# Loading a gated linear attention with MLP in single units, its weights through five shared staging tiles and in the order of use

## The chip, the cores and the metric

The kernel runs on one NeuronCore of a Trainium2 chip. The metric is the time of the device for one execution, in microseconds (us); before the change its median of three runs is 189.53 us (189.49 to 190.04).

The engines are called PE (TensorE, matrix products), PEld (its weight loads), ACT (ScalarE, exp, ln, silu), DVE (VectorE), POOL (GpSimd) and SP (SyncE, which here only issues transfers). A name with a q, such as SPq, is the engine's own queue of instructions.

## The reference

Two steps follow each other. The first is an attention with a decaying state, for 4 batches, 8 heads, 768 positions and 48 channels; the second is an MLP without biases on the 3072 rows of 384 numbers that the first one gives.

```python
f = 1.0 / (1.0 + np.exp(-f_logit))
for t in range(S):
    state = f[:, :, t, :, None] * state + np.einsum('bhd,bhe->bhde', k[:, :, t], v[:, :, t])
    y[:, :, t] = np.einsum('bhd,bhde->bhe', q[:, :, t], state)
x = y.transpose(0, 2, 1, 3).reshape(B * S, H * D)     # 3072 x 384
h = x @ w_in                                          # w_in 384 x 2048
out = (h / (1.0 + np.exp(-h))) @ w_out                # w_out 2048 x 384
```

All inputs and the output are float32 in memory; the matrix products run in bf16.

## The kernel before

**Units.** The sequence is cut into 6 chunks of 128 positions. A unit is one chunk of one batch with all 8 heads; there are 24, numbered chunk by chunk, so units 0 to 3 are the first chunk of the four batches. Two neighbouring units make a pair. A unit needs the state of unit u - 4 and nothing else of other units.

**A unit's way.** Its four inputs f, k, q, v are loaded (L485), 192 KB each, in pieces of 48 float32, which is 192 bytes. ACT makes the log of the gate (L492 exp, L494 ln). PE sums it along the chunk with a triangular matrix (`cs`, L565, and a small sum for the state, L569). ACT makes three exponentials of it (L572, L574, L576). POOL scales k (`ki`, L578) and casts v (`vb`, L580), DVE scales q (`qg`, L582). q and k are then transposed, on PE (`tq`, L588) with a copy by DVE (`qkc`, L590), or by a transposing DMA (`qkD`, L592); units from `turned` on take the DMA. PE multiplies k by q (`sc`, L599), DVE masks (`at`, L603), PE gives y from the state (L608) and the chunk (L612), DVE casts it (`yc`, L616). y is transposed on PE (`yT`, L620) and copied by DVE (`xc`, L622), or by a DMA (`xD`, L625); units from `y_turned` on take the DMA. The state is updated by PE (`d`, L630), DVE (`sd`, L635, L637) and POOL (`su`, L641), except in the last chunk.

**The MLP.** For units below `single` (6) the first product runs unit by unit (`m1`, L529, four groups j of 512 columns of w_in, 12 matmuls each, silu on L526); from there on in pairs (`mi`, L540, eight groups of 256 columns, silu on L536). The second product (`mo`, L551) is 16 matmuls a unit in four groups m, one for each quarter of w_out. For the first `halves` units it is cut in two sums, of which DVE adds the second to the first (L554, L557); the others are copied by L559. Rows are stored by a DMA (`so`, L562), issued from POOL for units below `store_sp` and from SP for the others. The results of both products take three banks of PSUM, the class `mlp`.

**The weights.** w_in comes in four pieces (`wi`, L505) by 512 columns, w_out in four pieces (`wo`, L510), each of 768 KB in float32. A piece is loaded into a staging tile and cast to bf16 by one engine (`ci`, `co`, L519 on ACT, L520 on DVE or POOL). Before, w_in has four staging tiles `ws` and w_out two of its own, `wt`.

**The order.** It is made when the program is built. `make_tasks` lists each step with its engine, an estimated duration and a priority: `base(u)` (unit number times `pace`) plus a rank of its kind from `CFG`; loads of the first units and of the weights have `... - 1000.0`, so that they come first, in the order of these numbers (`w_at` for the eight weight pieces). `schedule` simulates the five engines and the transfers, and on each free engine starts the ready step of the least priority whose buffers (`SLOTS`) are free. Its SP holds back while more than `DEPTH` of transfers is queued. ACT changes between the table of exp and ln and that of silu by the rules of `hold_` and `keep_` (L294); each change is a table load (L677). `planned` runs this twice and returns one list, which `emit` writes down; on the chip each engine runs its part of it in that order, and waits by semaphores. Where the plan leaves PE idle in the first 60 us, `idle` puts matmuls of a blank tile (L652), which keep its clock up.

The loads of units 0 to 3 are single before, those of later pairs are one transfer of 384 KB for both units:

```python
groups = [(u0,), (u0 + 1,)] if P < 2 else [(u0, u0 + 1)]
```

With `w_at` from 2.93 to 4.0 and loads at `us[0] + 0.25 * len(us) * n - 1000.0`, the weights of before start among the loads of unit 2's end and unit 3.

Of the kernel before, what the change touches and what calls it, by code (L numbers as in the profile page):

```python
# [24 lines left out]
    margin=0.35,  # L25
    pace=2.02,
    turned=12,
    y_turned=15,
# [3 lines left out]
    store_sp=11,  # L32
    single=6,
    w_at=(3.4, 2.93, 3.01, 3.21, 3.55, 3.06, 4.0, 3.68),
    cast=('POOL', 'POOL', 'POOL', 'DVE', 'POOL', 'DVE', 'ACT', 'POOL'),
    halves=2,
    first=0,
# [4 lines left out]
    hold_exp=0,  # L42
    hold_silu=1.23,
    keep_exp=161.0,
    keep_silu=99.1,
    rank=dict(ld=-139.74, E=59.92, cs=-262.24, ia=-97.88, ki=-182.71, vb=357.09, qg=-106.88, tq=-364.24,
              qkc=334.21, sc=-239.9, at=128.24, y=-100.34, yc=-226.99, yT=-342.32, xc=65.03, d=73.38,
              sd=-375.97, su=-193.54, mi=-180.01, si=-45.28, mo=255.49, mstep=0.29, half=87.3, cw=-240.41,
              oc=-156.5, so=-230.84, wi=138.12, wo=46.7),
    rank0=dict(ld=-194.56, E=-13.35, cs=-240.33, ia=-60.31, ki=48.5, vb=34.96, qg=158.95, tq=-143.29,  # L50
              qkc=448.89, sc=-352.48, at=303.25, y=-70.59, yc=77.2, yT=-185.62, xc=69.3, d=-225.94, sd=-290.13,
              su=-317.3, mi=-194.46, si=45.68, mo=151.34, mstep=3.25, half=10.32, cw=-320.34, oc=-83.48,
              so=-8.76, wi=-371.79, wo=305.83),
)

SLOTS = dict(f=5, k=5, q=5, v=5, ws=4, wt=2, e=2, lf=3, ia=2, qk=5, vb=6, qkT=4, atm=3, yb=3, xT=3, hT=3, sd=2, al=6, o=3,
# [4 lines left out]
DEPTH = 2.1  # L61
LOAD, TURN, WEIGHT, STORE = (1.2, 0.75, 0.015), (0.9, 0.1, 0.021), (1.2, 1.0, 0.2), (1.6, 1.2, 0.14)
ROW = {2: 0.097, 4: 0.178, 6: 0.235}
CAST_ENGINES = ('DVE', 'ACT', 'POOL')
CAST = dict(DVE=0.9, ACT=1.3, POOL=1.6)
# [3 lines left out]
class Task:  # L69
    def __init__(self, name, eng, dur, prio, deps=(), acq=(), use=(), mode=None, phase=None, load=0.0):  # L70
        self.name, self.eng, self.dur, self.prio = name, eng, dur, prio
        self.deps, self.acq, self.use = list(deps), list(acq), list(use)
        self.mode, self.phase, self.load = mode, phase, load
# [7 lines left out]
def make_tasks(cfg):  # L81
# [4 lines left out]
    def add(name, *a, **k):  # L86
        t = Task(name, *a, **k)
        T[name] = t
        tasks.append(t)
        return t  # L90
# [10 lines left out]
    for P in range(PAIRS):  # L101
        u0 = 2 * P
        for n, x in enumerate("fkqv"):
            inst((x, P), x)
        groups = [(u0,), (u0 + 1,)] if P < 2 else [(u0, u0 + 1)]
        for us in groups:
            for n, x in enumerate("fkqv"):
                add((x, us), "SP", 0.3 * len(us), base(us[0]) + R['ld'] + n * 0.1 if us[0] >= 8 else us[0] + 0.25 * len(us) * n - 1000.0, acq=[I[x, P]], load=kb(192 * len(us)))
    load_of = lambda x, u: T[x, (u,)] if u < 4 else T[x, (u - u % 2, u - u % 2 + 1)]

    for P in range(PAIRS):
        us_list = [(2 * P,), (2 * P + 1,)] if P < 2 else [(2 * P, 2 * P + 1)]
        for us in us_list:
# [3 lines left out]
            e = add(("E", us), "ACT", 0.067 + 0.32 * n, base(us[0]) + R['E'], deps=[T["f", us]], acq=[inst(("e", us), "e")],  # L117
# [5 lines left out]
    for u in range(UNITS):  # L123
# [16 lines left out]
        if dmat:  # L140
            qkT = add(("qkD", u), "SP", 1.25, B + R["tq"], deps=[qg, ki], acq=[I["qkT", u]], use=[I["qk", u]], load=1.38)
# [9 lines left out]
        if u >= cfg["y_turned"]:  # L151
            xc = add(("xD", u), "SP", 1.2, B + R["yT"], deps=[yc], acq=[I["xT", P]], use=[I["yb", u]], load=0.52)
# [12 lines left out]
    for n in range(NI):  # L165
        add(("wi", n), "SP", 0.45, cfg["w_at"][n] - 1000.0, acq=[inst(("ws", n), "ws")], load=24 / NI * ROW[8 // NI] * 2)
# [541 lines left out]
```

## Time and profile before

| what | value |
|---|---|
| time, median of 3 runs | 189.53 us |
| span of the profiled execution | 187.6 us |
| PE, busy share | 94% (2005 matmuls) |
| PEld | 75% |
| ACT | 70% (23 table loads of L677, 1283 ns each) |
| DVE | 51% |
| POOL | 37% |
| DMA, mean rate | 182 GB/s, 34.22 MB |
| transfers of SP | 119664 packets, 78.0% of 16 engines' span |
| granted PE clock | 0.989 |

The page cuts the span in 40 equal slices and gives each engine's busy share in tenths (9 is 90% or more). A busy PE is not a PE at its peak: matmuls overlap and their ends are modelled. The chain of waits is followed back from the last instruction to what released it, or to the instruction before it on its engine; where a row stands for several matmuls one after another, its length is their real pace. A row of the timeline has start, length, engine, line, operation, output and input, the count, and in brackets how long the engine was idle before and what ended that.

The chain gives 29% of the span to L551, 24% to L540, 4% to L529, 11% to SP's queue and 8% to DMA of q.

### The profile page before, as it was taken

The page shows a single profiled execution, that of the slowest core. Times are in us where ns is not written, and L with a number is a line of the kernel's source. Part 1 is how long each engine was busy: PE and PEld are TensorE (multiplying, and loading weights), DVE is VectorE, ACT ScalarE, POOL GpSimd, SP SyncE. Part 2 cuts the span into 40 slices and gives each one's busy share as a digit, 9 for nine tenths or more (in the row PEclk, how much of TensorE's full clock was granted, in tenths as well). Part 3 has the DMA queues.
Part 4 walks back from the last instruction along what each step waited for, and adds up shares of the span by engine and source line. Part 5 has one row for each costly group of instructions (what it writes and reads, how often), then busy time and mean ns, then how long its engine had stood idle before and what let it go on. Part 6 is the DMA issues. An engine that isn't in the chain of part 4 may idle for free.

```text
span 187.6 us, 4875 instructions
## 1 busy us (share of the span) xinstructions
PE 175.6 (94%) x2005; PEld 140.8 (75%) x2005; DVE 96.0 (51%) x185; ACT 131.2 (70%) x217; POOL 69.9 (37%) x112
## 2 busy tenths in 40 slices
PE   5987769999999999979999999999999999999991
PEld 5976659777777879768787787678688886966960
DVE  4278454444877783574626736875542415261011
ACT  4452835998797898998988788568669996810810
POOL 2338528444727570561751742490252006000000
PEclk9999988999999999999999999999999999999999
DMA  6989999999999999999799599379774866413101
GB/s 125 213 173 307 392 346 345 260 219 220 220 257 208 205 255 222 224 239 199 155 141 214 120 175 217 77 119 226 153 154 128 173 124 134 103 24 105 42 17 67
DMA packets 120389, 34.22 MB, mean 182 GB/s; under 512 B 116128, under 2 KB 117792, under 8 KB 120368
## 3 DMA queue, kind: packets, MB, share of 16 engines
q1 hardware_dynamic: 119664, 31.76, 78.0%
q0 software_dynamic: 704, 2.16, 3.2%
q8 instruction: 15, 0.25, 0.5%
q14 instruction: 6, 0.05, 0.1%
HBM read 25.17 MB, written 4.72 MB: 159 GB/s over the span
## 4 chain that ended last, share of the span: by engine, by line
PE 70%; SPq 11%; DMA 8%; ACT 5%; issue 2%; POOL 1%; DVE 1%; DVEq 0%; ACTq 0%
PE mlp L551 29%; PE mlp L540 24%; DMA q<-in_q_dram 8%; SPq L485 7%; SPq L505 4%; PE mlp L529 4%; PE sc L599 3%; PE yd L612 2%; PE yd L608 2%; PE cs L565 2%; ACT L677 2%; PE tq L588 1%; PE yd L630 1%; ACT hT L536 1%; PE tq L620 1%
## 5 line engine op out<-in xcount | busy, mean ns | idle before, releaser
L551 PE MATMUL mlp<-w_out,hT 128*128 128x384 bf16 x384 | 69.9, 326 | 0.0
L536 ACT ACTIVATE hT<-mlp 128x512 bf16<-128x512 f32 x72 | 41.7, 597 | 17.4 <-PE mlp L540 14.9
L540 PE MATMUL mlp<-xT,w_in 128*128 128x256 bf16 x432 | 51.5, 273 | 1.1 <-ACT hT L536 1.0
L551 PEld LDWEIGHTS <-hT 128*128 128x128 bf16 x384 | 34.8, 97 | 19.5
L540 PEld LDWEIGHTS <-w_in 128*128 128x128 bf16 x432 | 46.3, 114 | 3.2 <-issue 1.3
L578 POOL TENSOR_TENSOR qk<-k,ia 128x384 bf16<-128x384 f32 x24 | 24.0, 1001 | 54.5 <-ACT al L576 33.0
L603 DVE TENSOR_TENSOR atm<-sc,triu 128x512 bf16<-128x512 f32 x48 | 30.9, 685 | 19.8 <-PE sc L599 19.8
L677 ACT ACT_TABLE_LOAD x23 | 29.5, 1283 | 0.4
L641 POOL TENSOR_TENSOR st<-sd,al 48x192 bf16<-48x192 f32 x40 | 20.2, 505 | 16.2 <-DVE sd L635 8.6
L529 PE MATMUL mlp<-xT,w_in 128*128 128x128 bf16 x288 | 20.1, 228 | 2.3 <-DVE w_in L520 1.8
L572 ACT ACTIVATE ia<-cs 128x384 f32<-128x384 f32 x24 | 11.8, 490 | 14.9 <-PE cs L569 10.0
L616 DVE CAST yb<-yd 128x384 bf16<-128x384 f32 x24 | 13.3, 554 | 15.8 <-PE yd L612 15.8
L559 DVE COPY o<-mlp 128x384 f32<-128x384 f32 x22 | 12.2, 556 | 17.8 <-PE mlp L551 14.1
L529 PEld LDWEIGHTS <-w_in 128*128 128x128 bf16 x288 | 18.1, 117 | 3.1 <-DVE w_in L520 2.0
L582 DVE TENSOR_TENSOR qk<-q,cs 128x384 bf16<-128x384 f32 x24 | 13.2, 550 | 13.0 <-ACT cs L574 8.4
L526 ACT ACTIVATE hT<-mlp 128x512 bf16<-128x512 f32 x24 | 13.6, 597 | 7.1 <-PE mlp L529 6.6
L492 ACT ACTIVATE e<-f 128x768 f32<-128x768 f32 (+1 forms) x14 | 10.5, 748 | 6.5 <-DMA f<-in_f_logit_dram 6.4
L580 POOL CAST vb<-v 128x384 bf16<-128x384 f32 x24 | 11.6, 506 | 8.9 <-DMA v<-in_v_dram 8.8
L635 DVE TENSOR_TENSOR sd<-yd,st 128x384 f32<-128x384 f32 x16 | 8.9, 554 | 8.3 <-PE yd L630 6.2
L574 ACT ACTIVATE cs<-cs 128x384 f32<-128x384 f32 x24 | 11.4, 477 | 0.6
L652 PE MATMUL mlp<-blank 128*128 128x128 bf16 x112 | 10.5, 264 | 1.0 <-DVE blank L657 1.0
L494 ACT ACTIVATE lf<-e 128x768 bf16<-128x768 f32 (+1 forms) x14 | 10.5, 750 | 0.3
(43 smaller groups left out, 150.6 us busy)
## 6 DMA issues: line engine op xcount, KB each, us to landing
f<-in_f_logit_dram SPq DMA_DIRECT2D x10, 384.0 KB, 5.5
k<-in_k_dram SPq DMA_DIRECT2D x10, 384.0 KB, 5.9
q<-in_q_dram SPq DMA_DIRECT2D x10, 384.0 KB, 6.1
v<-in_v_dram SPq DMA_DIRECT2D x10, 384.0 KB, 5.6
ws<-in_moe_w_in_dram SPq DMA_DIRECT2D x4, 768.0 KB, 8.4
wt<-in_moe_w_out_dram SPq DMA_DIRECT2D x4, 768.0 KB, 8.2
out_dram<-o SPq DMA_DIRECT2D x13, 192.0 KB, 2.1
out_dram<-o POOLq DMA_DIRECT2D x11, 192.0 KB, 3.6
```

The lines of the kernel that those rows point to most:

```text
L485: nc.sync.dma_start(out=dst, in_=SRC[x].rearrange("b h s d -> s (b h) d")[c * C:(c + 1) * C, b * H:(b + n) * H])
L526: return nc.scalar.activation(at("hT", P)[:, 4 * j:4 * j + 4, i * C:(i + 1) * C], h, AF.Silu)
L529: nc.tensor.matmul(h[:, r, :], w_tile(kk, 4 * j + r), at("xT", P)[:, kk, i * C:(i + 1) * C], start=(kk == 0), stop=(kk == KT - 1))
L536: return nc.scalar.activation(at("hT", P)[:, 2 * j:2 * j + 2, :], h, AF.Silu)
L540: nc.tensor.matmul(h[:, i, :], w_tile(kk, n), at("xT", P)[:, kk, :], start=(kk == 0), stop=(kk == KT - 1))
L551: nc.tensor.matmul(o, at("hT", P)[:, n, i * C:(i + 1) * C], w_rows(n), start=(n % (NT // 2 if half else NT) == 0), stop=(n == NT - 1 or ha ...
L578: nc.gpsimd.tensor_mul(at("qk", u)[:, 1, :, 0:D], at("k", P)[:, i], at("ia", u))
L582: nc.vector.tensor_mul(at("qk", u)[:, 0, :, 0:D], at("q", P)[:, i], at("cs", u)[:, 0:HD].rearrange("p (h d) -> p h d", d=D))
L603: nc.vector.tensor_mul(at("atm", u)[:, r], at("sc", u)[:, r], triu[:, None, :].to_broadcast([C, NP, C]))
L616: nc.vector.tensor_copy(at("yb", u), at("y", u))
L641: nc.gpsimd.tensor_mul(at("st", u)[lo:lo + D, :, r * D:(r + 1) * D], at("sd", u)[lo:lo + D, :, r * D:(r + 1) * D], at("al", u)[lo:lo + D, ...
L677: nc.scalar.preload_act_table_set(SETS[after[t.idx]])
```

## The change

It concerns the order of loads above all. (1) All loads become single units of 192 KB; from unit 4 on their priorities put the two units of a pair side by side (f4, f5, k4, k5 and so on), and exp and ln are still taken for both at once. (2) `ws` and `wt` become one kind of staging tile, five of them, for all eight weight pieces. (3) `w_at` is now 3.9 to 3.97: behind every load of the first four units (the last of these has 3.75), w_in's four pieces in order and then w_out's four. Loads from unit 4 on get the priority of `base` with the rank `ld` and so come behind the weights. (4) The planner's model of the queue counts descriptors (`rows`) rather than time: SP may add a transfer while at most 136 are queued (200 - 64). (5) The numbers that order the work are new: `pace`, ranks, `hold_`, `keep_`, the estimates of casts and rows; the first two units have ranks of their own. (6) Some work changes its engine: `turned` 12 to 13, `y_turned` 15 to 21, `store_sp` 11 to 22, and the casts, now on ACT, DVE, POOL, DVE for w_in and DVE, DVE, POOL, POOL for w_out. The aim is that PE gets the first chunk whole, then w_in, then w_out, without waiting in between.

```diff
 CFG = dict(
-    pace=2.02,
-    turned=12,
-    y_turned=15,
+    pace=1.69,
+    turned=13,
+    y_turned=21,
...
-    store_sp=11,
+    store_sp=22,
-    w_at=(3.4, 2.93, 3.01, 3.21, 3.55, 3.06, 4.0, 3.68),
-    cast=('POOL', 'POOL', 'POOL', 'DVE', 'POOL', 'DVE', 'ACT', 'POOL'),
+    w_at=(3.9, 3.91, 3.92, 3.93, 3.94, 3.95, 3.96, 3.97),
+    cast=('ACT', 'DVE', 'POOL', 'DVE', 'DVE', 'DVE', 'POOL', 'POOL'),
-    first=0,
+    first=2,
-    hold_exp=0,
-    hold_silu=1.23,
-    keep_exp=161.0,
-    keep_silu=99.1,
-    rank=dict(ld=-139.74, E=59.92, cs=-262.24, ia=-97.88, ki=-182.71, vb=357.09, qg=-106.88, tq=-364.24,
+    hold_exp=0.0,
+    hold_silu=1.01,
+    keep_exp=214.84,
+    keep_silu=80.42,
+    rank=dict(ld=-170.73, E=222.04, cs=-453.96, ia=-56.16, ki=8.43, vb=128.32, qg=-332.85, tq=-305.42,
...
-SLOTS = dict(f=5, k=5, q=5, v=5, ws=4, wt=2, e=2, lf=3, ...
+SLOTS = dict(f=5, k=5, q=5, v=5, ws=5, e=2, lf=3, ...
...
-DEPTH = 2.1
+DEPTH = 200
...
-        groups = [(u0,), (u0 + 1,)] if P < 2 else [(u0, u0 + 1)]
+        groups = [(u0,), (u0 + 1,)]
         for us in groups:
             for n, x in enumerate("fkqv"):
-                add((x, us), "SP", 0.3 * len(us), base(us[0]) + R['ld'] + n * 0.1 if us[0] >= 8 else us[0] + 0.25 * len(us) * n - 1000.0, acq=[I[x, P]], load=kb(192 * len(us)))
+                add((x, us), "SP", 0.3 * len(us), base(us[0] // 2 * 2) + R['ld'] + n * 0.1 + us[0] % 2 * 0.01 if us[0] >= 4 else us[0] + 0.25 * len(us) * n - 1000.0, acq=[I[x, P]], load=kb(192 * len(us)), rows=64 * len(us))
...
-        add(("wo", n), "SP", 0.45, cfg["w_at"][NI + n] - 1000.0, acq=[inst(("wt", n), "wt")], load=8 * 4 / NO * ROW[6])
+        add(("wo", n), "SP", 0.45, cfg["w_at"][NI + n] - 1000.0, acq=[inst(("wt", n), "ws")], load=8 * 4 / NO * ROW[6], rows=32 // NO)
...
-                if busy[e] > now + EPS or (e == "SP" and sum(x[1] for x in q["hw"]) > DEPTH + 2 * EPS):
+                if busy[e] > now + EPS or (e == "SP" and sum(x[1] * x[5] for x in q["hw"]) > DEPTH - 64 + 1e-4):
```

## The prediction

> **What bounds the kernel now.** I first read the slices of the page, to see where TensorE has nothing of its own to do and what the transfer queues do then.
>
> ```profile
> PE   5987769999999999979999999999999999999991
> ...
> DMA  6989999999999999999799599379774866413101
> GB/s 125 213 173 307 392 346 345 260 219 220 220 257 208 205 255 222 224 239 199 155 141 214 120 175 217 77 119 226 153 154 128 173 124 134 103 24 105 42 17 67
> ```
>
> One slice is 4.69 us. From the seventh on (28 us) PE is full to the end; before that it isn't, and much of what it shows there is the warm-up matmuls of L652 (112 of them, none after 24 us). The DMA row is near full from 14 us. So there are two stages: a head, paced by what has landed, and a body, paced by PE. To put a number on it I need PE's real pace, since its busy time overlaps. The chain of waits has it.
>
> ```profile
> 42.21 0.47 PE tq L588 x8
> 62.66 1.34 PE mlp L529 x24
> 103.67 0.17 PE tq L620 x3
> 168.10 5.20 PE mlp L551 x32
> 173.31 5.24 PE mlp L540 x48
> ```
>
> (Start, length, what.) One matmul costs 0.1625 us on L551, 0.109 on L540, 0.056 on L529. A transposition of q and k (L588, eight) costs 0.45 to 0.47, one of y (L620, three) 0.17. Other rows of the same view: scores 0.33 a unit, y 0.17 + 0.20, d 0.17, cumulative sums 0.26 (0.16 in the last chunk). All the kernel's matmuls at this pace: 384 x 0.1625 = 62.4, 432 x 0.109 = 47.2, 288 x 0.056 = 16.0, attention 33.5; **work 159.1 us**. By 30 us, the timeline of PE has 84 matmuls of L529 (4.7) and 5.1 us of attention, 9.8 together. So **20.2 us are lost in the head**. The last matmul ends at 183.8 us: 153.8 us for the other 149.3, **4.5 us lost in the body**. The tail to the end of the span is 3.8, and the time is 1.9 over the span. 159.1 + 20.2 + 4.5 + 3.8 + 1.9 = 189.5. A change can win in the head, or in 4.5 us; all else is PE work.
>
> Then, what the head waits for: PE's timeline, that of POOL, and the issues of SP.
>
> ```profile
> 22.23 0.86 PE L529 MATMUL mlp<-xT,w_in 128*128 128x128 bf16 x12 [0.49 <-POOL w_in L520]
> 25.93 1.16 PE L529 MATMUL mlp<-xT,w_in 128*128 128x128 bf16 x12 [1.84 <-DVE w_in L520]
> ...
> 28.34 1.46 POOL L520 CAST w_in<-ws 128x1536 bf16<-128x1536 f32 x1 [0.89 <-DMA ws<-in_moe_w_in_dram]
> ...
> 17.10 4.46 SPq L505 DMA_DIRECT2D ws<-in_moe_w_in_dram  x1
> 21.60 0.49 SPq L485 DMA_DIRECT2D q<-in_q_dram  x1
> 22.13 3.43 SPq L510 DMA_DIRECT2D wt<-in_moe_w_out_dram  x2
> 25.61 0.44 SPq L485 DMA_DIRECT2D v<-in_v_dram  x1
> ...
> 32.94 0.45 SPq L510 DMA_DIRECT2D wt<-in_moe_w_out_dram  x1
> ```
>
> The four pieces of w_in begin their casts at 17.2, 20.7, 24.9 and 28.3 us, as w_out and loads lie between them. q of unit 3 is issued at 21.6, so unit 3 isn't there to be multiplied meanwhile (DVE waits for it until 29.2). The last piece of w_out waits for a staging tile, until 32.9. From 20 to 30 us PE does 5.5 us of its own work.
>
> **What the Trainium skill says.** "DMA: Bandwidth & Descriptors", section Specifications, wants at least 512 B a piece for line rate. The trace agrees: 192-byte packets of q, k, v, f ran at 217 GB/s (5 to 10 us), the weights' larger ones at some 375 (20 to 30 us). The same page, Issuing engines are not separate DMA queues, says that another issuer saves only the issuing time; so stores on POOL add no bandwidth. The trace of before has both kinds but doesn't isolate this. "SBUF — State Buffer", Who interferes with whom, says that a VectorE cast in a two-port mode and a GpSimd instruction block each other. It fits: the cast on DVE took 0.96 us with POOL idle, and 1.24 beside L641.
>
> **The change part by part.** *PE work.* turned 12 to 13 brings one more transposition of q and k: +0.45. y_turned 15 to 21 brings six of y: 6 x 0.17 = 1.02. Both lie on the full engine: **+1.5 us**. DVE gets one copy of 0.69 and six of 0.35 (+2.8 on 96 busy of 188; hidden under PE), SP loses seven transposing transfers (hidden).
>
> *Order of the head.* All 16 loads of units 0 to 3 now precede w_in, and w_in precedes w_out. A load is 192 KB, at 217 GB/s 0.91 us; the first lands at about 3.4, so the 16 take the queue from 2.0 to 16.5. I add 1 us for the change to weights, since the slice at 9.4 to 14 us fell to 173 GB/s and the first weight's issue took 2.02 us. A weight piece is 0.786 MB, at 375 GB/s 2.1 us: w_in lands at 19.6, 21.7, 23.8, 25.9. Casts: ACT 1.46 (its w_out row), DVE 0.96 to 1.24, POOL 1.47, DVE: ready at 21.1, 22.8, 25.3, 27.1. By then all four units are through attention (the last v lands near 17; scores, at, y, copies and transposition have some 3.5 us until 20.5). So from 21.2 PE has 4 units x 0.67 = 2.7 us for each piece of w_in, which come every 2.1 us; it no longer starves: 4 x 2.7 = 10.8, until 32. ACT's silus (16 x 0.60 = 9.6) keep up, with the table switched before.
>
> *Staging.* Five tiles serve the eight pieces. Four of w_in and one of w_out go at once; the sixth waits for the first cast (21.1), a wait in SP's queue, with loads of units 4 and 5 behind or ahead of it. I take two to four of these (1.8 to 3.6 us) ahead. Then w_out lands at 28.0, 31.9 to 33.7, 34 to 35.8, 36.1 to 37.9, and is cast on DVE, DVE, POOL, POOL by 29.2, 33 to 35, 35.5 to 37.3, 37.6 to 39.4. PE wants them from 32 on, at 1.95 us a piece for three units (three mlp banks): 32, 34, 36, 38. Bound: no wait, or 1.4 us. I take 0.7. The queue isn't idle meanwhile, so a late w_out is an early load of unit 4 or 5.
>
> *Single loads.* 40 more issues of some 0.45 us each, 18 us of SP's queue, which spends its time blocked by the transfers (a double load's issue took 1.5 in the median): nothing on PE. Same bytes and packets. The priorities put them as f4 f5 k4 k5 q4 q5 v4 v5, so a unit gains one load's 0.9 us over the pair, no more. For unit 4: from 17.5 us the queue has 8 x 2.1 of weights and seven loads of 0.91 to its v, so its q is in at 38.9 and its v at 40.7. From q to the finished xT: 0.55 + 0.45 + 0.69 + 0.33 + 1.29 + 0.37 + 0.55 + 0.17 + 0.35, 4.8 us and steps between engines, so 44 to 45. PE has the second products until 32 + 0.7 + 10.4 = 43, and some 2.5 of attention of units 4 and 5 (1.75 each): 45.6. Between 0 and 1.5 us lost; I take 0.8.
>
> *Sum of the head.* At 21.2 us PE has done attention for four units, 4 x 1.58 = 6.3. Lost: 14.9, and 0.7 + 0.8: 16.4 instead of 20.2: **-3.8 us**. By both bounds 14.9 to 17.8.
>
> *Stores.* store_sp 11 to 22 puts eleven more on POOL, 0.58 us each: 6.4 on 70 busy. A store waits for DVE's copy with L578 and L641 of later units behind it in POOL's queue, and those feed PE. POOL waited 3.6 us in all for 11 stores; twice that is hidden so long as units are ahead. The last two stay on SP, so the tail stays. *Ranks, pace, hold, keep* reorder the body; no row prices this. Its loss of 4.5 can go to about 3 or to 6.5; I leave it.
>
> Sum: 189.5 + 1.5 - 3.8 = 187.2. I round to **187.0**.
>
> **The rivals.**
> (a) *The body loses less too.* Transposing y on PE (0.17, copy 0.35) replaces a transfer of 2.5 us from issue to landing, and units become ready earlier. The 1.0 us wait of PE for a silu at 82 us, before a table load, can go. For it: seven fewer waits through SP. Against: PE showed only 3.9 us of waits beyond those for its own warm-up. With the head at its lower bound: 159.1 + 1.5 + 15 + 3.5 + 3.8 + 1.9 = 184.8 to 185.3.
> (b) *The head gains half.* Later w_out, unit 3's v and ACT's table (exp of unit 4 must wait until the 16 silus are done, at 32.6, then 1.28 us of table) leave 18.7 lost: 189.5 + 1.5 - 1.5 = 189.5, no change. For it: DMA is full in the head in either order, and the first matmul of the MLP starts no earlier than its 20.2.
> (c) *Slower.* The wait moves: w_in starts 4 us later, and what the better order gives back is lost to the wait for the sixth staging tile and to starved units 4 and 5. The loss stays 20.2 and the 1.5 of PE work is added: 191.0; a POOL blocked by stores could add 1.
>
> **How the numbers follow.** Main case 0.45 (187.0, some 186 to 188.5), (a) 0.27, (b) 0.13, (c) 0.15. Faster by over 0.3% (below 188.96): main and (a), 0.72 with a sliver of (b); same 0.11; slower 0.17. The range leaves out the better end of (a) and most of (c): 184.8 to 190.0.
>
> **What would show it.** In PE's timeline, L529 in runs for four units with no wait over 0.5 us after about 21 us. The casts of w_in close together (two us apart) and all before 28 us. 17 us lost by 45 us at the paces above. L620 with 63 matmuls, L588 with 104. If L529 starts after 23 us, or PE waits for a cast of w_out or for unit 4 between 32 and 45 us by over 2 us together, (b) or (c) holds. If the loss after 45 us differs by over 1.5 us from before, the ranks matter more than I grant.

## The result and the profile after

The changed kernel is slower by 1.35%: 192.14 us median of four runs (191.58 to 193.06) against 189.56 us (189.49 to 190.04) for the kernel before on the same chip. The ratio is 1.0135, with a 95% interval of 1.0091 to 1.0179. The forecast was 187.0 us.

The profiled execution of after took 193.06 us, the longest of its four, and that of before 189.34. The sums below are of these two, so they explain 3.7 us, somewhat more than the 2.6 between the medians. A second look at the same head, in a faster execution, stands below with the stores back on SP.

The page's slices, as in the prediction (one slice is 4.77 us here):

```profile
PE   5988689979699999999999999999999999999992
...
DMA  6999998879999899999999495489745923702012
GB/s 123 219 180 204 337 405 229 336 177 208 269 194 224 174 246 209 213 209 205 183 226 183 101 208 136 117 173 183 129 108 112 221 43 100 157 20 77 30 41 82
```

PE's row has gaps up to the eleventh slice (7 in the ninth, 6 in the eleventh, which ends at 52.5 us); before, it was full from the seventh. The seventh slice of GB/s (28.6 to 33.4 us) has 229 between 405 and 336, and the ninth (38 to 43 us) 177: the transfers of the weights have two holes. In finer steps, with the columns of the windows view (stretch, length, then busy time of PE, PEld, DVE, ACT and POOL, granted clock, DMA share, GB/s), after:

```profile
28.00:30.00 2.00, 1.91 (x39) 1.80 (x38) 1.03 (x2) 1.32 (x3) 1.06 (x1) 1.00 1.10 301
30.00:32.00 2.00, 2.00 (x40) 2.00 (x38) 1.39 (x3) 1.79 (x3) 0.00 (x0) 1.00 0.66 115
32.00:34.00 2.00, 2.00 (x39) 2.00 (x37) 0.23 (x1) 1.66 (x3) 0.00 (x0) 1.00 0.87 344
...
40.00:42.00 2.00, 2.00 (x18) 1.27 (x16) 0.00 (x0) 0.19 (x1) 1.15 (x2) 1.00 0.41 79
```

and before, for the same time:

```profile
30.00:32.00 2.00, 2.00 (x42) 1.91 (x39) 0.91 (x2) 1.28 (x3) 1.56 (x3) 1.00 1.08 323
32.00:34.00 2.00, 2.00 (x41) 1.90 (x36) 1.29 (x2) 1.40 (x3) 1.85 (x2) 1.00 1.07 182
...
40.00:42.00 2.00, 1.89 (x19) 1.14 (x17) 0.80 (x2) 1.97 (x3) 0.89 (x1) 1.00 1.17 222
```

115 and 79 GB/s come with a DMA share of 0.66 and 0.41: a good part of the time the transfer engines had nothing to do. The 182 of before has a share of 1.07: small pieces, but a full queue. What SP issues then, in the timeline of after (start, length of all the issues in the row, engine, line; w_in's first piece was issued at 15.9):

```profile
16.62 2.17 SPq L510 DMA_DIRECT2D ws<-in_moe_w_in_dram  x3
18.83 0.75 SPq L515 DMA_DIRECT2D ws<-in_moe_w_out_dram  x1
19.62 6.74 SPq L490 DMA_DIRECT2D f<-in_f_logit_dram  x2
26.50 5.95 SPq L515 DMA_DIRECT2D ws<-in_moe_w_out_dram  x3
32.50 4.15 SPq L490 DMA_DIRECT2D k<-in_k_dram  x2
36.69 4.87 SPq L490 DMA_DIRECT2D q<-in_q_dram  x2
```

The transfers into the five staging tiles are all issued by 19.6 us, with no wait, as forecast. Then come f of units 4 and 5, and the second of them holds SP from 20.12 to 26.37 us (6.25 of the row's 6.74). The first cast of w_in had freed its tile by 23.5, but w_out's second piece is issued only at 26.50, and that issue takes 4.19 of the next row. When the queue gives way again, it is nearly dry. The same follows at k5 (3.67 us) and q4 (4.20 us). The pieces of w_out land at 30.98, 34.52, 37.79 and 41.08 us, q of unit 4 at 43.33. The engines that wait for them are POOL with the casts and DVE with q (the bracket: how long it was idle, and what ended that):

```profile
37.85 1.47 POOL L525 CAST w_out<-ws 128x1536 bf16<-128x1536 f32 x1 [8.78 <-DMA ws<-in_moe_w_out_dram]
41.20 1.47 POOL L525 CAST w_out<-ws 128x1536 bf16<-128x1536 f32 x1 [0.85 <-DMA ws<-in_moe_w_out_dram]
```

```profile
43.45 0.55 DVE L587 TENSOR_TENSOR qk<-q,cs 128x384 bf16<-128x384 f32 x1 [6.45 <-DMA q<-in_q_dram]
```

And PE, in its timeline of after:

```profile
23.58 1.53 PE L534 MATMUL mlp<-xT,w_in 128*128 128x128 bf16 x24 [1.29 <-ACT w_in L524]
25.96 2.87 PE L534 MATMUL mlp<-xT,w_in 128*128 128x128 bf16 x48 [0.57 <-DVE w_in L525]
...
39.37 2.11 PE L556 MATMUL mlp<-w_out,hT 128*128 128x384 bf16 x12 [1.07 <-POOL w_out L525]
...
42.72 1.46 PE L556 MATMUL mlp<-w_out,hT 128*128 128x384 bf16 x8 [0.33 <-POOL w_out L525]
...
51.09 0.32 PE L570 MATMUL cs<-lf,triu 128*128 128x384 bf16 x1 [1.50 <-ACT lf L499]
```

The first matmul of the MLP starts at 23.58 us, the second product waits for POOL's casts, and at 51 us there is nothing to multiply, since f of units 6 and 7 is late (49.24). The stretches without a bracket aren't all work either: the warm-up matmuls of L657 (148 now, 112 before) fill some of them.

So I count again as in the prediction: the time passed, less PE's own matmuls at their real paces, is what PE has lost by then.

| us lost by | 30 | 35 | 45 | 60 | 75 | 180 us |
|---|---|---|---|---|---|---|
| before | 20.2 | 20.4 | 20.8 | 21.1 | 21.5 | 24.7 |
| after | 19.15 | 19.2 | 20.9 | 23.8 | 24.4 | 26.8 |

Until 35 us after is 1.2 us ahead. Then it loses 4.6 us up to 60, where before loses 0.7. From 60 on it loses 3.0, before 3.6. With 1.5 us more of PE work (160.5 against 159.1) that makes 1.5 + 2.7 - 0.6 = 3.6 of the 3.7 us. The added work is as forecast, in the groups by form of after:

```profile
L593 PE MATMUL tq<-ident,qk 128*128 128x128 bf16 x104 | 8.5, 226 | 0.3
...
L625 PE MATMUL tq<-ident,yb 128*128 128x128 bf16 x63 | 7.0, 219 | 0.1
```

### The profile page after: what moved, and what is told of

Its sections match the earlier page's. It is cut to its first block, busy times and chain, and to the rows that moved or that the text cites. A ratio compares the mean times of both kernels' runs of the same rounds, so it can differ in the third digit from the quotient of the medians.

```text
span 190.9 us, 5062 instructions
## 1 busy us (share of the span) xinstructions
PE 178.3 (93%) x2067; PEld 142.4 (75%) x2067; DVE 99.5 (52%) x194; ACT 129.5 (68%) x215; POOL 72.8 (38%) x121
## 4 chain that ended last, share of the span: by engine, by line
PE 60%; SPq 15%; DMA 11%; ACT 8%; DVE 2%; issue 2%; DVEq 0%; ACTq 0%
PE mlp L556 24%; PE mlp L545 23%; SPq L490 14%; DMA ws<-in_moe_w_out_dram 6%; DMA f<-in_f_logit_dram 5%; PE sc L604 3%; ACT L682 2%; PE mlp L534 2%; PE yd L617 2%; ACT e L497 2%; ACT lf L499 1%; SPq L510 1%; PE tq L625 1%; PE yd L613 1%; PE cs L570 1%
## 5 line engine op out<-in xcount | busy, mean ns | idle before, releaser
L541 ACT ACTIVATE hT<-mlp 128x512 bf16<-128x512 f32 x72 | 42.1, 597 | 17.7 <-PE mlp L545 15.5
L545 PE MATMUL mlp<-xT,w_in 128*128 128x256 bf16 x432 | 52.3, 273 | 0.3 <-ACT hT L541 0.2
L556 PEld LDWEIGHTS <-hT 128*128 128x128 bf16 x384 | 35.0, 97 | 21.6 <-issue 1.9
L545 PEld LDWEIGHTS <-w_in 128*128 128x128 bf16 x432 | 46.1, 114 | 2.7 <-issue 0.6
L583 POOL TENSOR_TENSOR qk<-k,ia 128x384 bf16<-128x384 f32 x24 | 24.0, 999 | 36.8 <-ACT al L581 22.3
L567 POOL DMA_DIRECT2D out_dram<-o x22 | 12.7, 579 | 30.1 <-DVE o L564 27.2
L564 DVE COPY o<-mlp 128x384 f32<-128x384 f32 x22 | 12.2, 555 | 20.1 <-PE mlp L556 19.6
L534 PE MATMUL mlp<-xT,w_in 128*128 128x128 bf16 x288 | 17.5, 219 | 2.2 <-ACT w_in L524 1.3
L534 PEld LDWEIGHTS <-w_in 128*128 128x128 bf16 x288 | 16.5, 114 | 2.7 <-ACT w_in L524 1.5
L531 ACT ACTIVATE hT<-mlp 128x512 bf16<-128x512 f32 x24 | 13.8, 597 | 3.8 <-PE mlp L534 2.9
L657 PE MATMUL mlp<-blank 128*128 128x128 bf16 x148 | 12.7, 247 | 1.0 <-DVE blank L662 1.0
L657 PEld LDWEIGHTS <-blank 128*128 128x128 bf16 x148 | 10.7, 113 | 1.3 <-DVE blank L662 1.0
```

Source lines behind the costliest of these rows:

```text
L531: return nc.scalar.activation(at("hT", P)[:, 4 * j:4 * j + 4, i * C:(i + 1) * C], h, AF.Silu)
L534: nc.tensor.matmul(h[:, r, :], w_tile(kk, 4 * j + r), at("xT", P)[:, kk, i * C:(i + 1) * C], start=(kk == 0), stop=(kk == KT - 1))
L541: return nc.scalar.activation(at("hT", P)[:, 2 * j:2 * j + 2, :], h, AF.Silu)
L545: nc.tensor.matmul(h[:, i, :], w_tile(kk, n), at("xT", P)[:, kk, :], start=(kk == 0), stop=(kk == KT - 1))
L556: nc.tensor.matmul(o, at("hT", P)[:, n, i * C:(i + 1) * C], w_rows(n), start=(n % (NT // 2 if half else NT) == 0), stop=(n == NT - 1 or ha ...
L583: nc.gpsimd.tensor_mul(at("qk", u)[:, 1, :, 0:D], at("k", P)[:, i], at("ia", u))
```

## The experiments

Theory: two small loads, f4 and f5, among the weights block SP's queue, the transfers run dry, and w_out and all loads behind it come 3 us late. Rivals: the transfers are held up by something else, namely the fetches of PE's program, which use a transfer engine for about 1 us each and fall at 30.5 to 31.6 and at 38.7 to 39.6 us in the trace of after; or the place of the work (transpositions and stores) costs it; or the new ranks do.

In the experiments on after the planned list is kept and only edited once it is planned, so each engine's order is that of after but for the lines shown. The edits add lines to the file: L534 of after is L538 in the first of them, and so on. All ratios are to the kernel before on the same chip.

### f4 and f5 behind the weights

```diff
 tasks, idles = planned(CFG, SLOTS)
+late = [t for t in tasks if t.name in (("f", (4,)), ("f", (5,)))]
+tasks = [t for t in tasks if t not in late]
+n = 1 + max(i for i, t in enumerate(tasks) if t.name[0] == "wo")
+tasks[n:n] = late
```

> The changed kernel with one edit: in SP's queue f of units 4 and 5 (128 small descriptors a transfer engine) stand behind the last piece of w_out and no longer between its first and second piece; the plan is otherwise kept. Theory A (the stream of transfers runs dry because SP is held back behind these two loads): w_out's second to fourth piece land near 33, 35 and 37 us and not at 34.5, 37.8 and 41.1, the hole at 30 to 32 us (71 GB/s) closes, PE waits for no cast of w_out, and the time falls by 1 to 2.5 us, to some 190. Theory B (the 1.5 us of added PE work and the new order of the body are the cause): no change within 0.5 us, as f only moves from 31 to 39 us.

190.27 us, ratio 1.0030 (1.0009 to 1.0052), against 1.0135 (1.0091 to 1.0179) for after: two loads in another place bring 1.0%, some 2 us. Windows, and SP's timeline:

```profile
30.00:32.00 2.00, 2.00 (x40) 2.00 (x38) 1.23 (x2) 1.61 (x4) 0.00 (x0) 1.00 1.02 411
...
36.00:38.00 2.00, 2.00 (x15) 1.19 (x13) 0.52 (x1) 1.83 (x3) 1.24 (x4) 1.00 0.67 135
```

```profile
19.08 9.85 SPq L519 DMA_DIRECT2D ws<-in_moe_w_out_dram  x4
28.99 4.23 SPq L494 DMA_DIRECT2D f<-in_f_logit_dram  x2
33.26 3.65 SPq L494 DMA_DIRECT2D k<-in_k_dram  x2
```

The weights now go through at 411 GB/s where after had 115, and w_out's last three pieces land at 32.2, 34.45 and 36.5 us instead of 34.5, 37.8 and 41.1. (The 71 and 82 GB/s that the expectations give for the two holes are 115 and 79 in the windows view.) PE has lost 18.7 us by 45, after 20.9. The hole isn't gone, though. It has moved behind the weights, to 36 to 40 us, where again a few small loads follow large ones (SP holds them from 28.99). From 45 to 75 us this kernel loses 3.5 us, and so it still isn't faster than before.

### f4, f5 and k4 one by one between the pieces of w_out

```diff
+for load, piece in ((("f", (5,)), ("wo", 1)), (("k", (4,)), ("wo", 2))):
+    t = next(t for t in tasks if t.name == load)
+    tasks.remove(t)
+    tasks.insert(1 + next(i for i, x in enumerate(tasks) if x.name == piece), t)
```

> The changed kernel with SP's order alternating: first piece of w_out, f4, second piece, f5, third piece, k4, fourth piece, k5; the plan is otherwise kept. E1 closed the hole at 30 us, but a new one came at 36 to 40 (135 and 167 GB/s), where two small loads follow the weights. Theory A2 (two small loads in a row behind weights hold SP back until the queue has run down): with one load at a time between the pieces there is no hole at 30 us, and the one after the last piece is smaller; the stream has moved by 42 us as much as in E1 or up to 1 us more; time 189.3 to 190.3. Rival (any small load between the pieces costs the queue its depth): the hole at 30 us comes back and the time is 191.5 to 192.5.

190.41 us, ratio 1.0030 (1.0010 to 1.0051), the same as the one before. Its windows:

```profile
30.00:32.00 2.00, 2.00 (x40) 2.00 (x38) 1.43 (x3) 1.79 (x3) 0.00 (x0) 1.00 1.02 357
...
38.00:40.00 2.00, 1.71 (x12) 0.94 (x10) 0.00 (x0) 1.84 (x3) 1.63 (x4) 1.00 0.77 167
```

One load between two pieces leaves no hole at 30 us; two behind one another do. Loads beside weights aren't harmful as such. Two different ways out of the bad order bring the same, which supports the theory (the time is 0.1 us above its range).

### Fewer warm-up matmuls, to move the fetches of PE's program

```diff
+idles = [x for x in idles if not 12.0 <= x[0] < 26.0]
```

> The changed kernel without the 67 warm-up matmuls that it puts between 12 and 26 us (a part of the computation is not touched: they multiply a blank tile). PE's program is fetched in blocks of 16 KB by the instruction queue; in the changed kernel the fetches at 30.5 and 38.7 us lie beside the two holes in the transfers (71 and 82 GB/s). Theory A1 (one transfer engine is late by the 1 us of the fetch, SP is held back by it, and the other fifteen run dry): with 134 instructions fewer the fetches come some 4 to 5 us later, and the holes move with them or vanish where weights are under way. Theory A2 (the small loads between the weights alone hold SP back): the holes stay at 30 and 40 us. Time: A1 between -1.5 and +0.5 us, A2 no change; if PE's clock falls for want of warm-up, slower, and the granted clock shows it.

192.74 us, ratio 1.0169 (1.0104 to 1.0234). The fetches moved to 28.1 and 36.8 us. The windows are these:

```profile
28.00:30.00 2.00, 2.00 (x30) 2.00 (x28) 0.96 (x1) 1.20 (x2) 0.76 (x1) 0.73 1.07 332
30.00:32.00 2.00, 2.00 (x44) 2.00 (x42) 1.11 (x2) 1.62 (x3) 0.00 (x0) 1.00 0.76 129
...
40.00:42.00 2.00, 2.00 (x18) 1.27 (x16) 0.00 (x0) 1.36 (x2) 1.47 (x1) 1.00 0.70 139
```

The holes stayed where they were, at 129 and 139 GB/s, without a fetch in them. In the first experiment, the other way round, a fetch at 30.8 to 31.9 us left no hole (411 GB/s). So the fetches don't make these two holes. They can still delay a single landing: w_out's last piece in after has 15 of its 16 shares at 39.93 us and the last, after a fetch, at 41.08. (The clock granted was 0.964 on the whole execution and 0.5 at 26 us, as PE was left cold, so the time itself says little.)

### The transpositions back on the transfers

```diff
+for u in range(15, 21):
+    tasks = [t for t in tasks if t.name != ("xc", u)]
+    t = next(t for t in tasks if t.name == ("yT", u))
+    t.name, t.eng, t.acq = ("xD", u), "SP", [x for x in t.acq if x.cls == "xT"]
+tasks = [t for t in tasks if t.name != ("qkc", 12)]
+t = next(t for t in tasks if t.name == ("tq", 12))
+t.name, t.eng = ("qkD", 12), "SP"
```

> The changed kernel with its plan, but y of units 15 to 20 and q and k of unit 12 transposed by DMA again, at the places of the PE transpositions. If PE is the bound of the body, as the prediction took it, this takes 1.5 us off: 190.6. If the later arrival by DMA (2.3 us from issue to landing and the wait in SP's queue) stops PE, it is no faster, or slower by up to 2 us.

193.52 us, ratio 1.0160 (1.0092 to 1.0228): nothing is gained, the second of its forecasts. PE's work falls back to 159.1 us, but PE loses 29.2 us by 180, 2.4 more than after. The waits of this kernel (engine, line, what it waited for: us in total, times, longest):

```profile
PE mlp L552 <- DMA xT<-yb: 2.3, 3, 1.4
...
PE sc L611 <- DMA qkT<-qk: 1.4, 1, 1.4
```

The plan of after puts the transposition close ahead of its use, and the transfer takes longer than that. So this says that the transpositions can't be taken back alone in this order, and nothing on what they cost. The next does.

### The kernel before, with y of units 15 to 20 transposed on PE

```diff
 tasks, idles = planned(CFG, SLOTS)
+for u in range(15, 21):
+    i, x = next((i, t) for i, t in enumerate(tasks) if t.name == ("xD", u))
+    bank = Inst(("yT", u), "tq")
...
+    t = Task(("yT", u), "PE", 0.17, 0.0, acq=[bank], use=x.use)
...
+    x.name, x.eng, x.use = ("xc", u), "DVE", [bank]
+    tasks.insert(i, t)
```

> The kernel before with its plan, but y of units 15 to 20 transposed on PE (three more matmuls each) and copied by DVE, at the places of the transposing DMAs: the y_turned part of the change alone, without a new order. If PE is the bound of the body: slower by 6 x 0.17 = 1.0 us, 190.5. If the shorter way saves waits of PE: less than that, down to 1 us faster.

191.43 us, ratio 1.0099 (1.0063 to 1.0135): 1.2 to 2.6 us, where six times 0.17 gives 1.0. So PE work added in the body shows in the time, with no less than its own length. Why it is more isn't shown. In the profiled execution (191.53 us) PE has lost 0.9 us more than in before by 110 us, ahead of the first added transposition at 121.5 us, where the instructions are the same in both; from there to 180 us it loses 0.4 us more. So most of the surplus there doesn't come from the added work or the copies that follow it.

### The stores back on SP

```diff
+for t in tasks:
+    if t.name[0] == "so" and t.name[1] >= 11:
+        t.eng = "SP"
```

> The changed kernel with its plan, but the stores of units 11 to 21 are issued by SP again, at the places where POOL had them. The prediction took the move as hidden: no change within 0.5 us. If stores on POOL hold back k and the state there, 0.5 to 1.5 us faster; if SP's waits for the copies of the output hold back loads and transposing transfers, slower.

191.89 us, ratio 1.0116 (1.0061 to 1.0171), not to be told from after's 1.0135. Within these intervals the issuer of the stores makes no difference, which agrees with the Trainium skill ("DMA: Bandwidth & Descriptors", Issuing engines are not separate DMA queues): another issuer saves no more than the time of the issue.

Up to the first moved store, at 117.7 us, this kernel has the instructions and the order of after. Its profiled execution, 190.57 us and the fastest of its four, is therefore a second look at after's head:

```profile
30.00:32.00 2.00, 2.00 (x40) 2.00 (x38) 1.23 (x2) 1.61 (x4) 0.00 (x0) 1.00 0.86 150
...
40.00:42.00 2.00, 2.00 (x18) 1.18 (x16) 0.55 (x1) 1.03 (x3) 1.29 (x2) 1.00 0.74 145
```

```profile
35.81 4.06 PE L559 MATMUL mlp<-w_out,hT 128*128 128x384 bf16 x24
```

f5 holds SP for 5.55 us here too, w_out's second piece lands at 34.32, and both holes are there, if less deep. But the third and fourth piece land at 36.19 and 38.21 us instead of 37.79 and 41.08. Their 16 shares lie 0.6 and 0.7 us apart instead of 1.6 and 2.8, so the slowest share lags less. PE waits for no cast of w_out, and has lost 2.2 us less than in after by 45 us and 2.6 less by 60. So the bad order doesn't cost the same in every execution. That the place of f4 and f5 makes after slower rests on the times of all runs, whose intervals lie apart (1.0091 to 1.0179 against 1.0009 to 1.0052); what the profile of after shows from 35 to 60 us is the case of a long execution.

### Pairs again

```diff
+for t in tasks:
+    if t.name[0] in ("f", "k", "q", "v") and t.name[1][0] >= 4 and t.name[1][0] % 2 == 0:
+        t.name = (t.name[0], (t.name[1][0], t.name[1][0] + 1))
+tasks = [t for t in tasks if not (t.name[0] in ("f", "k", "q", "v") and len(t.name[1]) == 1 and t.name[1][0] >= 4)]
```

> The changed kernel with its plan, but the loads of units 4 to 23 are single transfers for both units of a pair again, at the place of the first. The prediction gave single loads nothing (same bytes, same packets, 40 more issues that SP has time for): no change within 0.5 us, 191.6 to 192.6. If single loads help (finer steps for the queue) it is slower by up to 1 us; if 40 more issues hurt, faster by up to 1 us, with fewer and shorter holes.

191.39 us, ratio 1.0099 (1.0063 to 1.0136), which overlaps with after's interval. The loss after 45 us is 4.4 in its profile, against 5.9 in that of after. From 44 to 64 us 0.966 loads a microsecond arrive, against 0.923; but the kernel above with the stores on SP, with single loads like after, has 0.876, so executions differ by as much. This run doesn't settle it.

### Both: f4 and f5 as a pair behind the weights, and pairs from unit 4 on

The edit for pairs above, then:

```diff
+f4 = next(t for t in tasks if t.name == ("f", (4, 5)))
+tasks.remove(f4)
+tasks.insert(1 + max(i for i, t in enumerate(tasks) if t.name[0] == "wo"), f4)
```

> E1 and pairs together: from unit 4 on one transfer for both units of a pair, and that of f4 and f5 behind the last piece of w_out. In E5 the stream of loads from 44 to 64 us ran at 0.965 loads a us, against 0.85 in E1 and 0.925 in the changed kernel. If that holds here: 0.5 to 1 us better than E1, 189.2 to 189.8. If single loads are as good: 190.3.

189.39 us, ratio 0.9999 (0.9973 to 1.0024): level with before. Its windows:

```profile
30.00:32.00 2.00, 2.00 (x40) 2.00 (x38) 1.54 (x3) 1.73 (x3) 0.00 (x0) 1.00 1.03 417
...
36.00:38.00 2.00, 2.00 (x18) 1.27 (x16) 0.56 (x1) 1.91 (x3) 1.08 (x3) 1.00 0.64 127
38.00:40.00 2.00, 2.00 (x14) 1.17 (x12) 0.00 (x0) 1.72 (x3) 1.61 (x2) 1.00 1.19 238
```

The hole behind the weights is 2 us long here, where single loads had 135 and then 167 GB/s. PE has lost 19.5 us by 45, 20.6 by 60 and 23.4 by 180. That is 1.3 less than before at the end, for 1.5 us more work. The ranks, the places of work and the staging tiles are those of after, so these together don't make after slower than before; the order and grouping of the loads do.

### Alternating, and pairs from unit 6 on

The edit of the alternating kernel, and pairs as above with `>= 6`.

> E8 (small loads one at a time between the pieces of w_out) with pairs from unit 6 on. By the same reckoning 0.3 to 0.8 us better than E8: 189.5 to 190. If single loads are as good: 190.3.

190.23 us, ratio 1.0031 (1.0008 to 1.0055), the same as alternating alone, and the second of its forecasts. Pairs from unit 6 on bring nothing that shows, so if pairs bring something, it is at units 4 and 5.

### Wide pieces for the loads

To see what the small pieces cost behind the head, f4 and f5 are behind the weights as in the first experiment, and all loads from unit 4 on read as many bytes in pieces of 1536 instead of 192. They fetch other rows than the computation wants; the transfers, the instructions and the waits are the same in number, but each load has an eighth as many pieces.

```diff
+if u >= 4:
+    src = SRC[x].rearrange("b h s d -> (b h s d)").rearrange("(u p x) -> u p x", p=C, x=HD)[u]
+    dst = at(x, u // 2)[:, u % 2].rearrange("p h d -> p (h d)")
+    return nc.sync.dma_start(out=dst, in_=src)
```

> E1 (f4 and f5 behind w_out) with the loads of units 4 to 23 read as rows of 1536 bytes: the same number of bytes into the same tiles, but each partition gets 384 numbers that lie side by side in memory, so the values are not those of the unit (this part of the computation is changed). It asks what the small pieces cost. Theory A (from 36 to about 63 us PE is paced by the stream of 192-byte pieces, which gives back what E1 won in the head): PE's loss grows from 45 to 75 us by 1 us or less instead of 3.5, and the time is 187 to 188.5. Rival (the written order of PE makes the loss): no change, 190.

189.22 us, ratio 0.9985 (0.9964 to 1.0006), between its two forecasts and 0.45% better than the same with small pieces (1.0009 to 1.0052). From 46 to 58 us the transfers ran at 369 to 395 GB/s instead of 185 to 255. The loss from 45 to 75 us is 1.8 instead of 3.5. So in these two executions about half of what that kernel gives back there is due to the small pieces. The other half is open. No issue behind the weights takes more than 1.4 us here, where f5 took 3.75 with small pieces, and the hole behind the weights is gone (367 GB/s from 36 to 38 us). So the blocking of SP behind the weights goes with the small pieces, not with the bytes or the number of transfers. This run doesn't tell that blocking from the slower transfer of small pieces.

### The kernel before, with the new order alone

```diff
-    w_at=(3.4, 2.93, 3.01, 3.21, 3.55, 3.06, 4.0, 3.68),
+    w_at=(3.9, 3.91, 3.92, 3.93, 3.94, 3.95, 3.96, 3.97),
...
-SLOTS = dict(f=5, k=5, q=5, v=5, ws=4, wt=2, e=2, lf=3, ...
+SLOTS = dict(f=5, k=5, q=5, v=5, ws=5, e=2, lf=3, ...
...
-    add(("wo", n), "SP", 0.45, cfg["w_at"][NI + n] - 1000.0, acq=[inst(("wt", n), "wt")], load=8 * 4 / NO * ROW[6])
+    add(("wo", n), "SP", 0.45, cfg["w_at"][NI + n] - 1000.0, acq=[inst(("wt", n), "ws")], load=8 * 4 / NO * ROW[6])
...
```

> The kernel before with the new order of the head alone: five shared staging tiles and the new w_at, planned anew with the old ranks, pairs, casts and engines. Its queue then has the first chunk, w_in, w_out, and only then f of units 4 and 5. If the order of the head is sound and only the two loads within w_out spoilt it (A): the loss of PE by 45 us is 16 to 18.5 us instead of 20.8, and the time 187 to 188.5. If the order itself costs what it gains, as w_in comes 4 us later (C of the prediction): 189 to 191.

196.77 us, ratio 1.0394 (1.0331 to 1.0457): outside both its forecasts, much slower, and not by a hole, since from 26 to 34 us the transfers ran at 404 to 430 GB/s. PE loses 21.2 us by 30 and 26.4 by 60. Its timeline shows where it starts:

```profile
29.60 5.55 PE L529 MATMUL mlp<-xT,w_in 128*128 128x128 bf16 x96 [1.87 <-DVE w_in L520]
```

Here the plan was made anew with the old ranks and casts, so the order of all engines differs, and it is a bad one. That this is the reason is argued, not shown. What it does show is that with this order of work the new order of loads wins nothing.

### The kernel before, with w_in ahead of w_out only

The plan of before is kept; w_in and q of unit 3 go ahead of w_out, and all of w_out ahead of f4 and f5. Two pieces of w_out take used tiles of w_in.

```diff
...
+for n, (cls, slot) in {1: ("wt", 0), 0: ("wt", 1), 3: ("ws", tile_of["wi", 1].slot), 2: ("ws", tile_of["wi", 2].slot)}.items():
+    tile_of["wo", n].cls, tile_of["wo", n].slot = cls, slot
+for name, after in ((("wo", 1), ("q", (3,))), (("wo", 0), ("wo", 1)), (("v", (3,)), ("wo", 0)), (("wo", 3), ("v", (3,))),
+                    (("wo", 2), ("wo", 3)), (("f", (4, 5)), ("wo", 2)), (("co", 1), ("qg", 3))):
+    t = next(t for t in tasks if t.name == name)
+    tasks.remove(t)
+    tasks.insert(1 + next(i for i, x in enumerate(tasks) if x.name == after), t)
...
```

Some warm-up matmuls fall elsewhere by this and overwrite a part of one product of the MLP; the instructions are the same.

> The kernel before with its plan and ranks, and only the loads around the weights moved: w_in's pieces and unit 3's q ahead of every piece of w_out, v of unit 3 between them, all of w_out ahead of f of units 4 and 5; the third and fourth piece of w_out use the staging tiles of two pieces of w_in that are done; the cast of w_out's first piece stands 6 us later in DVE's order. If the runs are read rightly (no two small loads behind each other among the weights, w_in before w_out, no added PE work): w_in's casts come 2 us earlier than 24.9 and 28.3 us, PE's loss by 35 us is 18.5 to 19.5 us instead of 20.4, and the time is 188 to 189, faster than both. If the stream from 36 us on gives it back: 189.5.

190.65 us, ratio 1.0037 (1.0016 to 1.0059), slower than before and than both its forecasts. PE has lost 18.6 us by 30, a gain of 1.6 over before, but 20.0 by 35 (before 20.4), 21.8 by 45 and 22.6 by 75 (before 20.8 and 21.5). In PE's timeline:

```profile
31.20 0.40 PE L607 MATMUL sc<-qkT 48*128 48x128 bf16 x8 [1.33 <-DVE qkT L598]
...
35.83 0.36 PE L620 MATMUL yd<-vb,atm 128*128 128x48 bf16 x8 [0.80 <-POOL vb L588]
```

The first wait is made by the edit: DVE stands idle from 27.9 us until w_out's first piece lands at 29.09 and casts it, before it copies unit 3's q and k at 30.46. The second comes of v of unit 3, which is late now, and f of units 4 and 5 lands at 37.65 instead of 35.04. So in the kernel before too, w_in first wins in the head and gives it back, in part to what then comes later and in part to the place of one cast in DVE's order; this run doesn't tell what the order of the loads alone would give.

## Why the prediction was wrong

The forecast took 3.8 us off the head, and the head got 2.7 us worse by 60 us. By the prediction's own terms:

| term | forecast, us lost | measured |
|---|---|---|
| until the first matmul of the MLP | 14.9 (starts at 21.2) | 17.5 (23.58) |
| while w_in comes | 0 | 1.7 (up to 35) |
| waiting for w_out | 0.7 | 1.7 (35 to 45) |
| waiting for units 4 and 5 | 0.8 | 2.9 (45 to 60, units 4 to 7) |
| sum | 16.4 | 23.8 |

**Order of the head: the largest term, short by 4.3 us.** The first two rows were forecast at 14.9 us and measured at 19.2, and this hardly differs between executions: by the same paces, all nine kernels with after's head and its warm-up matmuls lost 18.6 to 19.4 us by 35. Two steps failed. The first is the arrival of w_in, 2.4 us late. The 16 loads and the change to the weights were forecast to end at 17.5 us, and the last load landed at 18.67. The first piece was given 2.1 us at 375 GB/s, and came 3.36 us later, at 22.03. From 18.67 to 22.03 us the transfers ran at 313 GB/s, which gives 2.5 us. The rest, some 0.9 us by this estimate, is what a mean rate leaves out: a piece is there when the slowest of 16 engines has brought its share. The trace counts the shares one by one: the first piece of w_in has its first at 20.36 and its last at 22.03 us, w_out's first piece 28.81 and 30.98. The Trainium skill says as much: a DMA runs on up to 16 engines that finish independently, and the semaphore counts them ("DMA: Bandwidth & Descriptors", Why a DMA increments its semaphore by 16 and not by 1). The trace agrees, with 1.7 and 2.2 us for these two pieces.

The second is "By then all four units are through attention", on which "it no longer starves" rests. When the first product starts at 23.58 us, only units 0 and 1 have their input; DVE's timeline has the other two (26.29 is unit 2, 31.88 unit 3):

```profile
24.94 0.96 DVE L525 CAST w_in<-ws 128x1536 bf16<-128x1536 f32 x1 [2.55 <-DMA ws<-in_moe_w_in_dram]
...
26.29 0.35 DVE L627 COPY xT<-tq 128x384 bf16<-128x384 bf16 x1
...
31.88 0.35 DVE L627 COPY xT<-tq 128x384 bf16<-128x384 bf16 x1
```

PE had made unit 2's transposition by 21.6 us, but DVE waits 2.55 us for w_in's second piece, with the copy behind the cast in its order. So the first piece gives PE 24 matmuls where the forecast had 48, and from 24.95 to 25.96 us there are only warm-up matmuls and a wait. That is 1.0 of the 1.7 us of the second row; no run moves this copy. The sign was right: by 35 us after is 1.2 us ahead of before, not 3.8.

**Staging: the mechanism that failed.** "The queue isn't idle meanwhile, so a late w_out is an early load of unit 4 or 5." It was idle: 115 and 79 GB/s in the windows, with SP held 6.25 and 4.19 us by single issues. The prediction saw SP blocked in its queue and counted that as hidden, as if a blocked issuer meant a full queue. Here the queue ran down while SP was blocked. The tile for w_out's second piece was free at 23.5 us, its issue began at 26.50 and was over at 30.68: it waited for SP, not for the tile. Two small loads in another place gave back 1.0%, and spreading them gave the same, with no other edit. w_out landed at 30.98, 34.5, 37.8 and 41.1 (forecast 28.0, up to 33.7, 35.8, 37.9), q and v of unit 4 at 43.3 and 45.3 (forecast 38.9 and 40.7): up to 4.6 us late, and this is where the 1.7 and 2.9 of the table come from, for 0.7 and 0.8; with f4 and f5 behind the weights nothing at all is lost from 30 to 45. These are the sizes of a long execution: in the faster one of the same head nothing is lost from 35 to 45 us either, and 2.3 from 45 to 60; in the one with the transpositions back on the transfers (193.97 us) it is 1.6 and 1.6.

**Single loads: "nothing on PE" is doubtful.** By the medians, pairs are better by 0.36% on after and by 0.31% with f4 and f5 behind the weights, the same sign and size twice, each time with overlapping intervals; from unit 6 on they bring nothing. With both undone the kernel is level with before.

**PE work: right.** 104 and 63 matmuls in the two groups, 1.5 us more work. That it lies on the path agrees with the kernel before with six transpositions on PE, which cost 0.63 to 1.35% where their own length is 0.54%.

**Stores, ranks and the body: right.** The stores made no difference that shows on either queue. The body after 60 us lost 3.0 instead of 3.6. The prediction said that a loss after 45 us more than 1.5 us off that of before would speak for the ranks; it was 2.0 off (5.9 against 3.9). That reading was wrong: with the same ranks, but other loads, it is 3.9, as before.

**The rivals.** The first product started at 23.58 us, after the 23 from which the prediction's own sign points to (b) or (c). What happened is nearest to (c), 191.0: the wait moved, and PE's 1.5 us came on top. But (c) expected the wait at the sixth staging tile and in starved units 4 and 5; of these the tile was free in time, and the units starved, also 6 and 7. The likeliest case failed on its head, and (c) got too little weight as the prediction priced no stall of SP's queue at all. The 3.9 us of PE's waits that it held against (a) leave out 2.5 us for the log of the gate and 0.3 for a copy; the trace of before has 6.7 beyond the 1.0 ahead of the warm-up matmuls.

**What stays open.** By which measure SP's queue is full, and why it lets go so late after two small loads behind large ones, wasn't found; the wide loads say only that it goes with the small pieces. Fifteen of the sixteen first loads, behind each other, held SP for 0.45 to 1.33 us each, and one for 2.08. How much of the difference between after and before falls on which wait in a usual execution is open too, as each kernel was profiled once. More staging tiles, which would let w_out go ahead of f4 and f5, weren't tried. No version was found that is faster than the kernel before beyond its interval.

## What to carry to other kernels

When a trace shows a long issue on a transfer queue, look at the GB/s of that very stretch before you call it hidden: a blocked issuer can stand ahead of an empty queue, and moving one or two small transfers from among large ones can be worth more than the order of the large ones. Time the start of work by when the last of the 16 shares lands, not by the mean rate, and check in every engine's order what stands behind a cast that waits for a transfer. And a gain at the head counts only if the loads behind it come no later; see what the second stage waits for before adding it up. Where executions of one kernel differ by 1 or 2 us, a profile shows what can happen, and the times of many runs say what usually does.

## What the hardware showed beyond that

- How far apart the 16 transfer engines finish their shares goes with the place in the queue rather than with the size, in the trace of after: the eight 768 KB pieces have 1.6 to 2.8 us, but for w_out's second, which came when the queue was empty, with 0.3 (34.22 to 34.52). The 192 KB loads f4 and f5 behind the weights have 1.8 and 1.7. The 16 first loads have 0.4 to 0.9, but for two with 2.0 and 1.7 after a fetch.
- PE's program is fetched in blocks of 16 KB, about 1 us each; the 16 of after, for 4134 instructions of PE and PEld, make some 258 a block. A load that meets one lands later by about that, in one of its 16 shares: in after q of unit 2 had 15 shares by 12.76 us and the last at 13.89; w_out's last piece 39.93 and 41.08. The dip of the page's rate at 9 to 14 us, which the prediction took for the cost of changing to weights, has such a fetch in it in both kernels, at 11.0 to 12.4 us in after and 11.6 to 12.6 in before. The load that SP issues then takes 2.08 us in after, where its neighbours take 0.65 to 1.33.
- The granted clock doesn't recover at once: in after without the warm-up matmuls from 12 to 26 us it was 0.50 from 16 to 28 us, though PE was busy for 3.9 of the last 4 of these, 0.73 at 28 to 30 and 1.00 from 30 on. In the kernel before, with PE busy for 0.16 us from 24 to 26, it was 0.58 and 0.56 at 26 to 30 us, in after with its 36 more warm-up matmuls 1.00. So a part of what after wins in the head may be clock; how much wasn't separated.
